# K transposed by VectorE in a one-core decode step (sliding attention beside a squared-ReLU MLP), and one w2 row laid on half the partitions

## The chip, the core and the metric

The kernel runs on one core of a Trainium2 chip. The core has five engines that run their own instruction streams and wait for one another through semaphores: TensorE (PE, matmuls; its weight loads are listed as PEld), VectorE (DVE), ScalarE (ACT), GpSimd (POOL) and SyncE (SP, which here only issues loads). Sixteen DMA engines move data between the main memory and the on-chip memory SBUF; matmul results go to PSUM. The metric is device time in microseconds (us), as the median of several runs; lower is better.

## What is computed

For two sequences with one new token each: a layer norm, attention of 32 query heads over the last 2048 positions of a cache with 16 K/V heads, and an MLP with a squared ReLU; both read the same normed token, and both are added to the input.

```python
W = min(4096, max(256, Sk // 4))                  # Sk = 8192: W = 2048
xn = _layernorm(x, axis=-1)                       # x: (2, 1, 576), bf16
q = (xn @ wq).reshape(B, Sq, 32, 128)             # wq: (576, 4096)
k = repeat(k_cache[:, :, Sk - W:, :], 2)          # caches: (2, 16, 8192, 128)
v = repeat(v_cache[:, :, Sk - W:, :], 2)
p = softmax(einsum("bhqd,bhkd->bhqk", q, k) * 128 ** -0.5)
a = einsum("bhqk,bhkd->bhqd", p, v).reshape(B, Sq, 4096) @ wo
h = relu(xn @ w1 + b1)                            # w1: (576, 4608)
m = (h * h) @ w2 + b2                             # w2: (4608, 576)
out = x + a + m
```

## The kernel before

**Units.** The attention is cut into eight units, u = 0 to 7; a unit is one sequence with four K/V heads. Its K and its V are 2 MB each. In SBUF a K tile has 128 partitions (four heads by 32 groups of 64 positions) and in each partition 64 rows of 128 bf16 numbers. Two bf16 numbers next to each other are moved as one f32, so a row is 64 f32.

**Loads.** All large loads are issued by SP, and they run in the order of issue: K0, wq, K1, V0, K2, V1, K3 at the start; V2, K4 and so on from the loop, each as soon as its buffer is free. K and V tiles share six buffers (`kvpool`), taken in turn; wq, w1 and wo share one buffer (`wbig`). So K4 waits until unit 1's K has been transposed, V3 until unit 0's V has been used, and wo until the matmuls with w1 (`mlp_h`) are done. w2 is split in two halves (x = 0, 1) of 18 rows for each partition; the first half goes to `w2a`, the second to `w2b` (9 rows, in a K/V buffer) and to `w2c` in pieces of 6, 2 and 1 rows (`W2P`), the last loads of the kernel. The small loads of x, b1 and b2 are issued from ScalarE's queue.

**A unit's work** (`step(u)`, line 387). `transposes(u, g)` (line 258) runs eight times: four 128x128 f32 transposes on TensorE into PSUM, and one copy to SBUF, by ScalarE (line 270) or VectorE (line 272) in turn. `scores(u, t)` (line 274), for either half t of the K tile, is eight matmuls of 512 columns whose stationary tile has 32 columns; four of them stand beside one another in the array (`tile_position`) and write to different partitions of `sc_ps`. The stationary tile is a window into `qz`, in which q stands between zeros. A first matmul puts a very low number at scores of foreign heads. `softmax(u)` (line 288) takes the maximum of each partition (VectorE), the maximum over partitions (GpSimd's `partition_all_reduce`), the exponential (ScalarE) and a transpose in 32x32 blocks to `pT` (VectorE). `pv(w)` (line 314), for the unit w = u - 2, is sixteen matmuls; `pv_end(w)` (line 326) adds the four column groups on VectorE, and its inner `fin` does one more matmul, the division by the sum, and writes the output of the heads to `ws`.

**Order.** TensorE's instructions keep the order of the program: the helpers `matmul` and `transpose` (lines 93 and 96) pass each through `keep_in_program_order`. Those of VectorE, ScalarE and SP are ordered by the tile framework, which also places all semaphore waits. The program's order is: transposes of unit 0, `q_block` (line 226: q = xn @ wq, transposed and laid into `qz`), scores and softmax of unit 0, steps 1 to 6, `mlp_h` (line 356), loads of wo and w2, step 7, the values of units 6 and 7, and at last the output matmuls (`out_acc`): 128 with wo, 72 with `w2a`, 36 with `w2b`, 36 with `w2c`; then one copy and the store.

Of the kernel before, what the change touches and what calls it, by code (L numbers as in the profile page):

```python
# [16 lines left out]
def kernel(  # L17
# [14 lines left out]
    nc = tc.nc  # L32
# [17 lines left out]
    JG = 8  # L50
    NG = NJ // JG
# [5 lines left out]
    TG = NG // NT  # L57
    QZ = 2 * NC
    assert SR == 32 and NG % NT == 0

# [15 lines left out]
    W2P = [(9, 15), (15, 17), (17, 18)]  # L76
    R9 = 9
# [15 lines left out]
    def matmul(*a, **k):  # L93
        tc.keep_in_program_order(nc.tensor.matmul(*a, **k))  # L94

# [20 lines left out]
    def issue_flat(w, name):  # L116
        n = w.shape[0] * w.shape[1] // P
        tl = wbig.tile([P, NH * L1], BF16, tag="wbig", name=name)
        nc.sync.dma_start(out=tl[:, 0:n], in_=w.rearrange("r n -> (r n)").rearrange("(p l) -> p l", p=P))
        return tl  # L120

    const.tile([P, 144], F32, name="pad_0")
# [15 lines left out]
    tmp_f = work.tile([P, 2, Dh], F32, tag="tmp", name="tmp_f")  # L138
# [50 lines left out]
    nc.vector.tensor_scalar(out=off[:], in0=own[:], scalar1=BIG, scalar2=-BIG, op0=ALU.mult, op1=ALU.add)  # L189
    of_h = const.tile([P, NC * WC], F32, name="of_h")  # L190
# [20 lines left out]
    w2c_sb = w2pool.tile([P, (FR - R9) * D], BF16, name="w2c")  # L211
# [8 lines left out]

    qz = const.tile([P, NQ, B, 2, 3 * QZ], BF16, name="qz")
    nc.gpsimd.memset(qz[:], 0.0)
# [3 lines left out]
    def q_block():  # L226
        for t in range(NH):
            for g in range(NG4):
                o = t * LQ + g * QW
                matmul(q_ps[32 * g:32 * g + 2 * B, :], lhsT=xnT[:, t].rearrange("p x b -> p (x b)"),  # L230
                       rhs=wq_sb[:, o:o + QW], start=(t == 0), stop=(t == NH - 1), skip_group_check=True,
                       tile_position=(0, 32 * g))
        row_t = const.tile([RB, 4 * HW], BF16, tag="row", name="qrow")
        qrow = row_t[:, 0:2 * QW]
        nh = QH // 2
        for k in range(2):
            cp = nc.scalar.copy if k else nc.vector.tensor_copy
            cp(out=qrow[:, k * QW:(k + 1) * QW].rearrange("p (i a d) -> p i a d", a=2, d=Dh),  # L238
               in_=q_ps[0:RB, k * QW // 2:(k + 1) * QW // 2].rearrange("p (i d) -> p i d", d=Dh).unsqueeze(2)
               .to_broadcast([RB, nh, 2, Dh]))  # L240
        qrow_f = qrow.bitcast(F32)
        qT_ps = psum.tile([P, QH * P], F32, tag="sc", bufs=2, name="qT_ps")
        for i in range(QH):
            transpose(out=qT_ps[:, i * P:i * P + RB], in_=qrow_f[:, i * Dh:(i + 1) * Dh],
                      identity=ident_f[0:RB, 0:RB])
        qT_v = qT_ps[:].bitcast(BF16).rearrange("p (i g e x b c) -> p b x g c e i", g=NG4 // 2, e=2, x=32 // B, b=B, c=2)
        hd = Dh // 2
        for j2 in range(2):
            cp = nc.scalar.copy if j2 else nc.vector.tensor_copy
            pp = slice(hd * j2, hd * (j2 + 1))  # L250
            o = QZ + NC * j2
            for b in range(B):
                for half in range(2):
                    cp(out=qz[pp, half * NQ // 2:(half + 1) * NQ // 2, b, :, o:o + NC].rearrange(  # L254
                        "p g c (e i) -> p g c e i", e=2), in_=qT_v[pp, b, half])

    kT_tiles, sc_tiles, pT_tiles, o1_tiles, o_tiles = {}, {}, {}, {}, {}
    def transposes(u, g):
        k_f = k_tiles[u][:].bitcast(F32)
        kT_ps = psum.tile([P, JG * P], BF16, tag="kT", bufs=3, name=f"kT_ps_{u}_{g}")  # L260
        kT_f = kT_ps[:].bitcast(F32)
        for i in range(JG // 2):
            j = g * JG // 2 + i
            transpose(out=kT_f[:, i * P:(i + 1) * P], in_=k_f[:, j * P:(j + 1) * P], identity=ident_f[:])
        t, o = divmod(g, TG)
        if o == 0:
            kT_tiles[(u, t)] = ktpool.tile([P, TG * JG * P], BF16, tag="kT_sb", name=f"kT_{u}_{t}")
        kT = kT_tiles[(u, t)][:, o * JG * P:(o + 1) * JG * P]
        if g % 2 == 0:
            nc.scalar.copy(out=kT, in_=kT_ps[:])  # L270
        else:
            nc.vector.tensor_copy(out=kT, in_=kT_ps[:])  # L272

    def scores(u, t):
        tq, b = divmod(u, B)
# [4 lines left out]
        kT = kT_tiles.pop((u, t))[:].rearrange("p (j k c) -> p j k c", k=P, c=2)  # L280
        z = QZ * (1 - t)
        for c in range(2):
            for g in range(4):
                matmul(sc_ps[32 * g:32 * (g + 1), :], lhsT=qz[:, tq, b, c, z:z + SR],
                       rhs=kT[:, :, 32 * g:32 * (g + 1), c], start=False, stop=(t == NT - 1 and c == 1),
                       skip_group_check=True, tile_position=(0, 32 * g))

    def softmax(u):
        sc_ps = sc_tiles.pop(u)
        m1 = work.tile([P, 1], F32, tag="m1", name=f"m1_{u}")  # L290
        nc.vector.tensor_reduce(out=m1[:], in_=sc_ps[:], axis=AX.X, op=ALU.max)  # L291
        m2 = work.tile([P, NC], F32, tag="m2", name=f"m2_{u}")
        nc.vector.tensor_scalar(out=m2[:], in0=off[:], scalar1=m1[:, 0:1], scalar2=None, op0=ALU.add)  # L293
        gmax = work.tile([P, NC], F32, tag="gmax", name=f"gmax_{u}")
        nc.gpsimd.partition_all_reduce(gmax[:], m2[:], channels=P, reduce_op=ReduceOp.max)  # L295
        gown = work.tile([P, NC], F32, tag="gown", name=f"gown_{u}")
        bias = work.tile([P, 1], F32, tag="bias", name=f"bias_{u}")
        nc.vector.scalar_tensor_tensor(out=gown[:], in0=gmax[:], scalar=-scale, in1=own[:], op0=ALU.mult,  # L298
                                       op1=ALU.mult, accum_out=bias[:])
        p_sb = work.tile([P, NJJ * 32], BF16, tag="p_sb", bufs=1, name=f"p_{u}")  # L300
        o1 = keep.tile([P, Dh + 1], F32, tag="o1", name=f"o1_{u}")
        nc.scalar.activation(out=p_sb[:], in_=sc_ps[:], func=ACT.Exp, bias=bias[:, 0:1], scale=scale,  # L302
                             accum_out=o1[:, Dh:Dh + 1])
        pT = keep.tile([P, NJJ, SR], BF16, tag="pT", name=f"pT_{u}")
        nc.vector.transpose(out=pT[:].rearrange("p j r -> p (j r)"), in_=p_sb[:])  # L305
        pT_tiles[u] = pT
        o1_tiles[u] = o1
# [4 lines left out]
    nc.gpsimd.memset(hT_sb[:], 0.0)  # L312

    def pv(u, part, parts):
        n = NJJ // parts
        if part == 0:
            o_tiles[u] = psum.tile([P, NS * Dh], F32, tag="o", name=f"o_ps_{u}")
        v = v_tiles[u][:].rearrange("p (t j s d) -> p j t s d", t=NT, s=2, d=Dh)
        for j in range(part * n, (part + 1) * n):
# [3 lines left out]
        if part == parts - 1:  # L323
            pT_tiles.pop(u)

    def pv_end(u):
# [3 lines left out]
        for k in range(NS):  # L330
            kw = dict(out=o1[:, 0:Dh], in0=o_ps[:, k * Dh:(k + 1) * Dh])
            if k == 0:
                nc.vector.tensor_scalar(scalar1=in_s[:, 0:1], scalar2=None, op0=ALU.mult, **kw)  # L333
            else:
                nc.vector.scalar_tensor_tensor(scalar=in_s[:, k:k + 1], in1=o1[:, 0:Dh], op0=ALU.mult, op1=ALU.add,  # L335
                                               **kw)

        def fin():
# [5 lines left out]
            nc.vector.reciprocal(out=linv[pp, :], in_=op[pp, Dh:Dh + 1])  # L344
            om_t = work.tile([P, Dh], F32, tag="om", name=f"om_{u}")
            om = om_t[pp, :].rearrange("p (q r) -> p q r", r=WR)
            nc.vector.scalar_tensor_tensor(out=om, in0=op[pp, 0:Dh].rearrange("p (q r) -> p q r", r=WR),
                                           scalar=linv[pp, 0:1], op0=ALU.mult, op1=ALU.mult,
                                           in1=own_c[pp, :].unsqueeze(2).to_broadcast([32, WC, WR]))
            with nc.allow_low_precision(reason="sums of one term and zeros"):  # L350
                nc.vector.tensor_reduce(out=ws[pp, :, BS * b], in_=om.rearrange("p q r -> p r q"), axis=AX.X,
                                        op=ALU.add)
# [3 lines left out]
    def mlp_h(w1_sb):  # L356
        h_ps = [psum.tile([P, HB], F32, tag="kT", bufs=3, name=f"h_ps_{k}") for k in range(2)]
# [28 lines left out]

    def step(u):
        fin = None
        w = u - 2
        with_pv = w >= 0  # L390
        for g in range(NG):
            transposes(u, g)
            if with_pv and g == 1:
                pv(w, 0, 2)
            if with_pv and g == 2:
                pv(w, 1, 2)
                fin = pv_end(w)
            if g == TG + 1:
                scores(u, 0)
            if g == TG + 2 and fin:  # L400
                fin()
        scores(u, 1)
        softmax(u)

    def pv_all(u):
        pv(u, 0, 1)
        pv_end(u)()

    for g in range(NG):
        transposes(0, g)  # L410
    q_block()
    for t in range(NT):
        scores(0, t)
    softmax(0)
    load_v(2)
    b1_rows = B_b1.rearrange("(x n) -> x n", n=HW)
    for i0, i1 in ((0, 2), (2, 4), (4, 6), (6, 8)):
# [3 lines left out]
    load_k(4)  # L421
# [16 lines left out]
    nc.sync.dma_start(out=w2a_sb[:], in_=w2_rows[0])  # L438
# [10 lines left out]
    for r in range(FR):  # L449
        w, o = (w2b_sb, r) if r < R9 else (w2c_sb, r - R9)  # L450
        out_acc(hT_sb[:, 1, r, :], w, o, stop=(r == FR - 1))
# [36 lines left out]
```

## Time and profile before

| what | value |
|---|---|
| median of 7 runs | 133.96 us (133.94 to 134.53) |
| the profiled execution: its own time, its span | 133.98 us, 132.1 us |
| loads from main memory | 53.6 MB, 406 GB/s over the span |
| mean granted clock of TensorE | 0.84 of full speed |
| last wq byte landed, first scores | 19.1 us, 25.6 us |
| last K tile (unit 7) issued, transposed | 61.3 us, 108 us |
| wo issued, after the w1 matmuls | 95.0 us |
| last `ws` ready, end of the wo matmuls | 118.2 us, 122.0 us |
| `w2a`, `w2b`, first piece of `w2c` landed | 122.8, 125.9, 128.0 us |
| last matmul, end of the span | 129.3 us, 132.1 us |

The span is the time from the first to the last instruction in the trace of one execution; the time of that execution is some 2 us longer. A page shows the busy time of each engine, the span in 40 slices (each digit is a busy share in tenths), the chain of work that ended last, and groups of like instructions. In a group, the arrow shows output and inputs by the program's names; "x32" is the number of instructions; then come the busy time in us, the mean time of one in ns, and the idle time of the engine just before them with what ended it. [...]

### The profile page before, as it was taken

The numbers are of one execution on the slowest core, as the hardware profiler recorded it, in microseconds if no ns is written. First come the engines' busy times: TensorE is split into PE (matmuls) and PEld (weight loads), VectorE is DVE, ScalarE is ACT, GpSimd is POOL, SyncE is SP. The second block draws the span as 40 slices with busy tenths as digits, with TensorE's granted clock in tenths as the row PEclk, the third lists the DMA queues.
The fourth block names the chain that finished last, engine by engine and source line by source line (L and its number), as shares of the span: only waits on it lengthen the run. The fifth ranks groups of instructions, "written<-read, shape, count | busy, mean of one in ns | idle before, by whom it ended". The sixth has DMA issues, their size and how long they took to land.

```text
span 132.1 us, 2285 instructions
## 1 busy us (share of the span) xinstructions
PE 84.9 (64%) x949; PEld 52.0 (39%) x949; DVE 63.4 (48%) x176; ACT 46.7 (35%) x67; POOL 4.9 (4%) x15
## 2 busy tenths in 40 slices
PE   0079229599589687597599779304739974339561
PEld 0069102276345353263436435002436631128450
DVE  7764300345657677396527757620165377750000
ACT  5716300339576094373253376020206352000000
POOL 5000000010010100100100010100000001000000
PEclk9999985959999999999658999975775699856955
DMA  4999899999999999999999999999999999899960
GB/s 150 407 437 514 380 393 427 432 437 427 434 412 446 422 437 422 432 437 422 442 427 414 437 488 402 427 454 387 432 427 446 463 413 480 376 408 430 408 253 1
DMA packets 3511, 53.76 MB, mean 407 GB/s; under 512 B 419, under 2 KB 558, under 8 KB 814
## 3 DMA queue, kind: packets, MB, share of 16 engines
q1 hardware_dynamic: 3456, 53.61, 95.1%
q8 instruction: 7, 0.11, 0.3%
q10 hardware_dynamic: 46, 0.02, 0.1%
q14 instruction: 2, 0.02, 0.0%
HBM read 53.62 MB, written 0.00 MB: 406 GB/s over the span
## 4 chain that ended last, share of the span: by engine, by line
DMA 78%; PE 15%; ACT 2%; SPq 1%; DVE 1%; issue 1%; ACTq 0%; DVEq 0%
DMA w<-in_B_w_dram 25%; DMA w2c<-in_B_w_dram 24%; DMA k<-in_A_k_cache_dram 16%; DMA wq<-in_A_wq_dram 13%; PE kT_ps L97 5%; PE h_ps L94 3%; PE q_ps L94 3%; PE sc_ps L94 2%; PE out_ps L94 1%; PE o_ps L94 1%; ACT kT L270 1%; DVE qrow L238 1%; SPq L106 0%; ACT qrow L238 0%; DVE qz L254 0%
## 5 line engine op out<-in xcount | busy, mean ns | idle before, releaser
L97 PE MATMUL kT_ps<-ident_f,k 128*128 128x128 f32 x256 | 41.8, 313 | 6.4 <-DMA k<-in_A_k_cache_dram 4.1
L97 PEld LDWEIGHTS kT_ps<-ident_f,k 128*128 128x128 f32 x256 | 32.8, 161 | 21.2 <-issue 12.1
L270 ACT COPY kT<-kT_ps 128x1024 bf16<-128x1024 bf16 x32 | 31.9, 1012 | 20.4 <-PE kT_ps L97 20.2
L272 DVE COPY kT<-kT_ps 128x1024 bf16<-128x1024 bf16 x32 | 21.8, 682 | 6.3 <-PE kT_ps L97 6.1
L94 PE MATMUL sc_ps<-kT,qz 128*32 128x512 bf16 x128 | 10.3, 406 | 6.7 <-DVE kT L272 4.7
L302 ACT ACTIVATE p<-sc_ps,bias 128x512 bf16<-128x512 f32 x8 | 5.5, 687 | 21.4 <-DVE gown L298 21.4
L94 PE MATMUL o_ps<-v,pT 128*32 128x512 bf16 x128 | 11.4, 442 | 0.0
L94 PEld LDWEIGHTS <-xnT 128*4 128x4 bf16 x108 | 3.4, 115 | 15.4 <-issue 14.0
L305 DVE STREAM_TRANSPOSE pT<-p 128x512 bf16<-128x512 bf16 x8 | 5.7, 710 | 6.2 <-ACT p L302 6.2
L335 DVE SCALAR_TENSOR_TENSOR o<-o_ps,in_s,o 128x128 f32<-128x128 f32 x24 | 8.3, 345 | 0.4
L94 PE MATMUL h_ps<-w,xnT 128*4 128x288 bf16 x72 | 3.9, 397 | 6.8 <-DMA w<-in_B_w_dram 6.8
L291 DVE TENSOR_REDUCE m<-sc_ps 128x1 f32<-128x512 f32 x8 | 5.5, 692 | 5.3 <-PE sc_ps L94 5.3
L295 POOL PARTITION_ALL_REDUCE gmax<-m x8 | 2.9, 367 | 105.8 <-DVE m L293 105.8
L94 PE MATMUL q_ps<-wq,xnT 128*4 128x512 bf16 x36 | 3.8, 596 | 4.8 <-DMA wq<-in_A_wq_dram 4.8
L94 PE MATMUL op_ps<-o,of_h 128*32 128x129 f32 x16 | 3.4, 299 | 4.8 <-DVE o L335 4.8
L375 DVE TENSOR_TENSOR hrow<-t 100x1152 bf16<-100x1152 f32 x2 | 2.6, 1355 | 8.0 <-ACT t L373 8.0
L94 PEld LDWEIGHTS <-qz 128*32 128x32 bf16 x128 | 2.2, 96 | 10.5 <-DVE kT L272 7.2
L456 ACT CAST fin_sb<-out_ps 113x144 bf16<-113x144 f32 x1 | 0.3, 279 | 17.0 <-PE out_ps L94 17.0
L97 PE MATMUL pro_ps<-ident,xn_sb 2*128 2x2 bf16 x5 | 0.9, 181 | 6.8 <-DVE xn_sb L171 6.5
L333 DVE TENSOR_SCALAR o<-o_ps,in_s 128x128 f32<-128x128 f32 x8 | 2.7, 343 | 5.0 <-PE o_ps L94 4.9
L94 PEld LDWEIGHTS <-hT_sb 128*17 128x17 bf16 x144 | 3.5, 111 | 3.8 <-issue 3.7
L238 DVE CAST qrow<-q_ps 100x512 bf16<-100x512 f32 x1 | 0.7, 691 | 7.9 <-PE q_ps L94 7.9
(71 smaller groups left out, 58.1 us busy)
## 6 DMA issues: line engine op xcount, KB each, us to landing
k<-in_A_k_cache_dram SPq DMA_DIRECT2D x8, 2048.0 KB, 21.0
v<-in_A_v_cache_dram SPq DMA_DIRECT2D x8, 2048.0 KB, 21.5
w<-in_B_w_dram SPq DMA_DIRECT2D x1, 5184.0 KB
wq<-in_A_wq_dram SPq DMA_DIRECT2D x1, 4608.0 KB, 17.7
wo<-in_A_wo_dram SPq DMA_DIRECT2D x1, 4608.0 KB
w2a<-in_B_w_dram SPq DMA_DIRECT2D x1, 2592.0 KB, 27.3
w2b<-in_B_w_dram SPq DMA_DIRECT2D x1, 1296.0 KB
w2c<-in_B_w_dram SPq DMA_DIRECT2D x1, 864.0 KB
```

The lines of the kernel that those rows point to most:

```text
L94: tc.keep_in_program_order(nc.tensor.matmul(*a, **k))
L97: tc.keep_in_program_order(nc.tensor.transpose(*a, **k))
L238: cp(out=qrow[:, k * QW:(k + 1) * QW].rearrange("p (i a d) -> p i a d", a=2, d=Dh), in_=q_ps[0:RB, k * QW // 2:(k + 1) * QW // 2].rearrang ...
L270: nc.scalar.copy(out=kT, in_=kT_ps[:])
L272: nc.vector.tensor_copy(out=kT, in_=kT_ps[:])
L291: nc.vector.tensor_reduce(out=m1[:], in_=sc_ps[:], axis=AX.X, op=ALU.max)
L295: nc.gpsimd.partition_all_reduce(gmax[:], m2[:], channels=P, reduce_op=ReduceOp.max)
L302: nc.scalar.activation(out=p_sb[:], in_=sc_ps[:], func=ACT.Exp, bias=bias[:, 0:1], scale=scale, accum_out=o1[:, Dh:Dh + 1])
L305: nc.vector.transpose(out=pT[:].rearrange("p j r -> p (j r)"), in_=p_sb[:])
L333: nc.vector.tensor_scalar(scalar1=in_s[:, 0:1], scalar2=None, op0=ALU.mult, **kw)
L335: nc.vector.scalar_tensor_tensor(scalar=in_s[:, k:k + 1], in1=o1[:, 0:Dh], op0=ALU.mult, op1=ALU.add, **kw)
L375: nc.vector.tensor_tensor(out=h4[:, :, k * HB:(k + 1) * HB], in0=t4, in1=t4, op=ALU.mult)
```

## The change

**K is transposed by VectorE.** In `transposes(u, t)`, now called twice for a unit, one VectorE instruction turns half a K tile, 128 partitions by 2048 f32, in blocks of 32x32: within each group of 32 partitions, straight from SBUF to SBUF. TensorE's 32 transposes of a unit, their PSUM tiles and the eight copies are gone.

**Scores with a block-diagonal stationary tile.** After that, each group of 32 partitions holds other positions, and one matmul has to multiply each group by q alone. `own_p` marks the group of each partition. `q_block` lays q, four times over the partitions, into `qc`; for each unit `q_place(u)` multiplies `qc` by `own_p` into one of two tiles `qz`, which makes it block-diagonal. A stationary tile is now a 128-column window into `qz`, and `scores(u, t)` is eight matmuls over the whole array, with 512 columns each.

**The order on VectorE is written out.** VectorE's instructions of a unit go through `keep_in_program_order` (`dve`). In `step(u)`: `pv(u - 2)` and both halves of the scores on TensorE; on VectorE `pv_end(u - 2)`, the maxima of unit u, `fin`, `q_place(u + 1)`, the first transpose of unit u + 1, then `rest` (bias, exponential on ScalarE, `pT`), then the second transpose of unit u + 1.

**Loads.** K4 is loaded before step 1 instead of after it, b1 in eight loads instead of four; wq, w1, wo and `w2a` keep the order of the program. `w2b` holds 11 rows and `w2c` 6 (pieces of 3, 2 and 1). The 18th row of the second half of w2 goes to a tile `w2x` on partitions 0 to 63, two rows on each, in four loads between `w2a` and `w2b`; for it `mlp_h` makes the matching part of h (`hx_sb`) by one more transpose and three ScalarE copies, and eight output matmuls take the place of four.

The core of the diff:

```diff
-    W2P = [(9, 15), (15, 17), (17, 18)]
-    R9 = 9
+    R9 = 11
+    RL = FR - 1
+    W2P = [(R9, 14), (14, 16), (16, RL)]
+    PL = P // 2
...
+    dve = tc.keep_in_program_order
...
-    qz = const.tile([P, NQ, B, 2, 3 * QZ], BF16, name="qz")
-    nc.gpsimd.memset(qz[:], 0.0)
+    qc = const.tile([P, NQ, B, NA, NC], BF16, name="qc")
+    qz = [const.tile([P, NA, P + QO], BF16, name=f"qz_{k}") for k in range(2)]
+    for k in range(2):
+        nc.gpsimd.memset(qz[k][:], 0.0)
...
+        for h in range(2):
+            cp = nc.scalar.copy if h else nc.vector.tensor_copy
+            cp(out=qrow[:, h * 2 * QW:(h + 1) * 2 * QW].rearrange("p (i a d) -> p i a d", a=NP4, d=HD),
+               in_=q_v[:, h].unsqueeze(2).to_broadcast([RB, QH, NP4, HD]))
...
+    def q_place(u):
+        tq, b = divmod(u, B)
+        sh = [P, NA, NP4, NC]
+        dve(nc.vector.tensor_tensor(out=qz[u % 2][:, :, QO:].rearrange("p a (q c) -> p a q c", c=32)[:, :, :, 0:NC],
+                                    in0=qc[:, tq, b].unsqueeze(2).to_broadcast(sh),
+                                    in1=own_p[:].unsqueeze(1).unsqueeze(3).to_broadcast(sh), op=ALU.mult))
...
-    def transposes(u, g):
...
-        for i in range(JG // 2):
-            j = g * JG // 2 + i
-            transpose(out=kT_f[:, i * P:(i + 1) * P], in_=k_f[:, j * P:(j + 1) * P], identity=ident_f[:])
...
-        if g % 2 == 0:
-            nc.scalar.copy(out=kT, in_=kT_ps[:])
-        else:
-            nc.vector.tensor_copy(out=kT, in_=kT_ps[:])
+    def transposes(u, t):
+        kT = ktpool.tile([P, UE // NT], BF16, tag="kT_sb", name=f"kT_{u}_{t}")
+        n = UE // NT // 2
+        tc.keep_in_program_order(nc.vector.transpose(out=kT[:].bitcast(F32),
+                                                     in_=k_tiles[u][:].bitcast(F32)[:, t * n:(t + 1) * n]))
+        kT_tiles[(u, t)] = kT
...
-        for c in range(2):
-            for g in range(4):
-                matmul(sc_ps[32 * g:32 * (g + 1), :], lhsT=qz[:, tq, b, c, z:z + SR],
-                       rhs=kT[:, :, 32 * g:32 * (g + 1), c], start=False, stop=(t == NT - 1 and c == 1),
-                       skip_group_check=True, tile_position=(0, 32 * g))
+        for i in range(NS // NT):
+            z = QO - NC * (t * NS // NT + i)
+            for h in range(2):
+                for e in range(2):
+                    matmul(sc_ps[:], lhsT=qz[u % 2][:, 2 * h + e, z:z + P], rhs=kT[:, i, :, h, :, e], start=False,
+                           stop=(t == NT - 1 and i == NS // NT - 1 and h == 1 and e == 1), skip_group_check=True)
...
     def step(u):
...
+        if w >= 0:
+            pv(w)
+        for t in range(NT):
+            scores(u, t)
+        fin = pv_end(w) if w >= 0 else None
+        rest = softmax(u)
+        if fin:
+            fin()
+        if u + 1 < NU:
+            q_place(u + 1)
+            transposes(u + 1, 0)
+        rest()
+        if u + 1 < NU:
+            transposes(u + 1, 1)
...
+    q_place(0)
+    step(0)
     load_v(2)
+    load_k(4)
...
-    for i0, i1 in ((0, 2), (2, 4), (4, 6), (6, 8)):
+    for i0, i1 in tuple((i, i + 1) for i in range(8)):
...
+    w2_last = w2_rows[1, :, RL * D:FR * D].rearrange("(e i q j) n -> e i j q n", e=2, i=2, q=4)
+    for i in range(2):
+        for e in range(2):
+            nc.sync.dma_start(out=w2x_sb[32 * i:32 * (i + 1), e, :], in_=w2_last[e, i])
     nc.sync.dma_start(out=w2b_sb[:], in_=w2_rows[1, :, 0:R9 * D])
```

## The prediction, made before the changed kernel was run

> **What bounds the kernel now.** I read the page's first two parts, then the chain that ended last, then the timeline of one unit, then the groups by shape. The page's head and the chain in order of time (start us, us, what):
>
> ```profile
> span 132.1 us, 2285 instructions
> PE 84.9 (64%) x949; PEld 52.0 (39%) x949; DVE 63.4 (48%) x176; ACT 46.7 (35%) x67; POOL 4.9 (4%) x15
> DMA  4999899999999999999999999999999999899960
> ...
> 58.08 32.97 DMA w<-in_B_w_dram
> ...
> 96.35 31.57 DMA w2c<-in_B_w_dram
> ...
> 127.96 1.36 PE out_ps L94 x36
> ```
>
> No engine is full; the DMA row stands at 9 from the second slice to the last but one, and the chain is 78% DMA. The kernel is bound by its load stream: 53.6 MB at about 430 GB/s. One unit's K and V (4.19 MB) take 9.8 us of it, and the compute of a unit fits in. The slack is small at the end: the last `ws` is ready at 118.19, the 128 `wo` matmuls end at 122.0, and `w2a` lands at 122.8. A compute end some 3 us later takes the bound over. So the question is whether a unit still fits in 9.8 us when VectorE (DVE) does all the transposing. One unit's softmax now (start us, us):
>
> ```profile
> 45.47 0.37 POOL L295 PARTITION_ALL_REDUCE gmax<-m  x1 [8.59 <-DVE m L293]
> 45.87 0.17 DVE L298 SCALAR_TENSOR_TENSOR gown<-gmax,own 128x8 f32<-128x8 f32 x1 [0.57 <-POOL gmax L295]
> 46.17 0.69 ACT L302 ACTIVATE p<-sc_ps,bias 128x512 bf16<-128x512 f32 x1 [3.15 <-DVE gown L298]
> 46.98 0.71 DVE L305 STREAM_TRANSPOSE pT<-p 128x512 bf16<-128x512 bf16 x1 [0.93 <-ACT p L302]
> ```
>
> From `gown` to the end of pT it is 47.69 - 45.87 = 1.82 us, 0.93 of it DVE's wait for the exponential. The groups (busy us, mean ns):
>
> ```profile
> L97 PE MATMUL kT_ps<-ident_f,k 128*128 128x128 f32 x256 | 41.8, 313 | 6.4 <-DMA k<-in_A_k_cache_dram 4.1 <-ACT kT L270 2.2
> L270 ACT COPY kT<-kT_ps 128x1024 bf16<-128x1024 bf16 x32 | 31.9, 1012 | 20.4 <-PE kT_ps L97 20.2
> L272 DVE COPY kT<-kT_ps 128x1024 bf16<-128x1024 bf16 x32 | 21.8, 682 | 6.3 <-PE kT_ps L97 6.1
> L305 DVE STREAM_TRANSPOSE pT<-p 128x512 bf16<-128x512 bf16 x8 | 5.7, 710 | 6.2 <-ACT p L302 6.2
> L144 DVE STREAM_TRANSPOSE row<-tmp_f 128x32 f32<-128x32 f32 x1 | 0.2, 163 | 0.0
> L375 DVE TENSOR_TENSOR hrow<-t 100x1152 bf16<-100x1152 f32 x2 | 2.6, 1355 | 8.0 <-ACT t L373 8.0
> L238 DVE CAST qrow<-q_ps 100x512 bf16<-100x512 f32 x1 | 0.7, 691 | 7.9 <-PE q_ps L94 7.9
> ```
>
> **Removed.** 256 TensorE transposes (41.8 us), 32 ScalarE copies (31.9) and 32 DVE copies (21.8). None lies long on the chain, so this buys nothing by itself. DVE gives up 4 x 0.68 = 2.7 us a unit.
>
> **Added on DVE: two transposes of 128x2048 f32 a unit.** The trace has no such size. L238 to L375 gives DVE's pace: (1355 - 691)/(1152 - 512) = 1.04 ns an element. L305 carried on at that pace: 710 + 1536 x 1.04 = 2.30 us. The line through the two transposes (163 at 32, 710 at 512) has 1.14 ns and gives 2.46. As a floor, the L272 pace (682 for 1024) gives 1.36; as a ceiling, twice the pace from L144 gives 163 + 2016 x 2.08 = 4.36. I take 2.30, nearest the same operation, and 2.34 with the gap.
>
> [...]
>
> **DVE's order is now written out**, so a step is a sum. From the end of the second transpose of unit u: `pv_end`, four operations, 114.92 to 116.43 in the timeline, 1.51. Then the wait for the second eight score matmuls, below. m1 and m2, 0.69 + 0.23 + gaps, 1.0. `fin`, 0.16 + 0.35 + 0.40 + gaps, 0.97. `q_place`, 128 elements; the nearest row is L347 with 347 ns, 0.38 (bounds 0.2 to 0.5). First transpose 2.34. `rest`, 1.82 + 0.04. Second transpose 2.34. The POOL reduction hides under `fin` and the first transpose; the exponential is waited for, and behind pT stands the second transpose, for which TensorE waits. Without the scores wait: 1.51 + 1.0 + 0.97 + 0.38 + 2.34 + 1.86 + 2.34 = 10.4 us, already above 9.8.
>
> **The scores wait.** 32-column matmuls ran four beside each other; the new ones fill the array and run singly: 16 a unit, 512 columns each. `q_ps` ran four abreast in 3.76/9 = 0.42 us at granted clock 0.5, so one takes 0.42 at half clock and 0.21 at full. Eight and 0.2 of latency are 1.9 or 3.6 us, of which `pv_end` covers 1.5: the wait is 0.4 or 2.1. Which clock? Stretches (length, PE, PEld, DVE, ACT, POOL busy, clock, DMA share, GB/s):
>
> ```profile
> 60.05:63.46 3.41, 1.85 (x17) 0.75 (x15) 2.30 (x5) 1.01 (x1) 0.00 (x0) 1.00 0.99 423
> 63.46:66.87 3.41, 2.48 (x16) 1.71 (x16) 1.61 (x5) 1.73 (x3) 0.37 (x1) 0.50 1.00 428
> 66.87:70.29 3.42, 3.42 (x25) 1.88 (x18) 0.90 (x3) 1.07 (x2) 0.00 (x0) 0.50 1.04 434
> 111.26:114.67 3.41, 1.17 (x18) 0.57 (x18) 2.68 (x10) 0.78 (x2) 0.00 (x0) 1.00 0.94 405
> ```
>
> The clock changed at steps of 3.41 us: it fell after a stretch with 1.85 us busy, stayed low after 2.48, and came back after 3.42. In the new step TensorE at full clock has 8 x 0.21 + 0.2 scores, 0.4 `op`, 1.2 pv, then some 3 us of nothing until the first transpose, 2.1 of scores, and 2 of nothing. So the clock will fall in most steps, and return when the doubled work fills a stretch. I take the middle: a step of 11.6, between 10.8 and 12.5.
>
> [...]
>
> **The start.** `qrow` now has 1024 columns a half: DVE 0.69 + 512 x 1.04 = 1.22, ScalarE 1.01 by L270's row, one after the other as now: +0.95. Two more transposes +0.2; `q_place` +0.38; the first half's copies move under ScalarE's, -0.5. Scores of unit 0 begin at 25.64 + 1.05 = 26.7. Seventeen matmuls at full clock take 3.7, at half 7.2; the clock was 0.5 from 25.9 on, so I put the end at 33.6, against 27.3 now. Then 1.0 + 0.38 + 2.34 + 1.86 + 2.34 = 7.92: unit 1 transposed at 41.5. Step 1 has no `pv_end` to cover the wait (1.9 or 3.6, say 2.7): 41.5 + 2.7 + 7.92 = 52.1. Five steps of 11.6: unit 7 transposed at 110.1. K itself is there in time throughout (unit 7's at about 96).
>
> **The end.** `hrow` and its 2.63 us (95.34 to 97.97) fall among DVE's last steps. Scores 2.7. m1 to pT end 3.36 (109.76 to 113.12). To the last `ws` 5.07 (113.12 to 118.19). `wo` matmuls 3.6. The w2 matmuls, 148 for 144, by 1.05 + 0.77 + 1.26 + 1.34 = 4.42: 4.54. Sum 21.9: TensorE ends at 132.0 against 129.32, +2.7. With the 2.78 behind it the span is 134.8. Around the span lies 133.98 - 132.1 = 1.9, and 133.98 is the median (133.96) but for 0.02: 136.7.
>
> **Queues.** `wo` waits for the `w1` matmuls, which stand on TensorE behind step 6: transposed at 98.5, + 3.6 + 0.6, + 3.9 as now = 106.6. Loads queued behind w1 (landing 91.1) are 6.3 MB, dry at 105.7. The stream loses 1 to 3 us there and ends near 131: no more than the compute. K and V buffers come free later too (K of unit 5 issued at 52 instead of 42.9), but each stays some 10 us ahead of its place in the stream. Eight `b1` loads for four: 4 x 0.33 us on ScalarE's queue ahead of `rstd`; what follows from it is wanted at 19.1 and done by 8.4; without that cover 1.3. They also held SP's issues up (6.3 us in three waits), under 9 MB of loads queued since 2.25.
>
> **The w2 row.** Same bytes, four SP issues of 0.42 us, 25 us ahead of their data. In the last 1.3 us before 128.5 the DMA share is about 0.4: part of the engines are done. [...] Bounds -0.4 to +0.5 with small packets; only worth something while the stream is the bound, so 0 here. The extra `hx` transpose and three ScalarE copies (about 0.31 each) hide while DVE transposes unit 7; uncovered 1.2.
>
> **Rivals.** *The stream stays the bound* (0.35). One mechanism: clock at full in the first scores (-3) and in the steps (10.8: -4.0) brings the chain to 125 to 128, before the data; from 3 us on it decides. Then the w2 row and a steadier stream count: 132.8 to 134.2, likeliest 133.4, faster. For it: before.py's compute of a unit is only 9 us, K is always early, and half the steps may run at full clock. Against: 10.4 without any wait.
> *Half clock throughout* (0.12): steps of 12.5 add 4.5: 141.2. For it, the long idle stretches; against, doubled work fills them.
> *The f32 transpose runs at half pace* (0.03): 14 transposes stand after 33.6, x 2.06 = 29 us: 165. Against it: L144 leaves then only 96 ns fixed, below the 130 ns and more of other small operations.
> The forecast has 0.50. [...]
>
> **Numbers.** 136.7; faster 0.26, same 0.07 and slower 0.02 share the first rival's 0.35; slower is 0.50 + 0.12 + 0.03 + 0.02 = 0.67. A measurement of this kernel tells 0.2% from no change. Range 132.8 to 140.5: the first rival whole, steps up to 12.3; the likeliest case's own 134.5 to 139.
>
> **What will show it.** Transposes of 2.2 to 2.5 us, 16 of them; steps, from one second transpose to the next, of 10.8 to 12.5; DVE the largest share of the chain in place of DMA; the clock at 0.5 in much of 30 to 110; `wo` issued after 103; dips of the DMA row near slice 32. I am wrong if steps are under 10.5 or the chain is still mostly DMA.

## The result, and the profile after

The changed kernel takes 1.017 times the time of the kernel before (95% interval 1.0147 to 1.0193), 2.3 us more on 134.03. The profiled execution took 135.84 us. The median of all twelve executions, 138.16 us, includes some at a lower granted clock of TensorE (0.78 to 0.80 of full speed), which the comparison leaves out; 1.017 stands for about 136.3 us. So the change made the kernel slower, close to the 136.7 that was forecast, but much of the agreement is two errors that cancel, as the sections below show.

The page of the changed kernel, its head, the busy rows, the chain by engine and the new transposes:

```profile
span 134.0 us, 1753 instructions
...
PE 70.6 (53%) x702; PEld 31.0 (23%) x702; DVE 81.3 (61%) x169; ACT 16.4 (12%) x38; POOL 5.5 (4%) x17
...
PEclk9999999959999999689689689779975579755698
DMA  4999899999999999999999999999999999999920
...
DMA 35%; DVE 27%; PE 26%; ACT 4%; issue 4%; SPq 1%; ACTq 0%
...
L274 DVE STREAM_TRANSPOSE kT<-k 128x2048 f32<-128x2048 f32 x16 | 36.5, 2284 | 0.0
```

TensorE lost 14 us of work, ScalarE 30, and VectorE gained 18. The chain was 78% DMA before and is 35% now. The DMA row is still at 9 until the data are all there, near 128.7. Behind that TensorE works on: compute ends this kernel, not the stream. The clock row shows 6 8 9 three times from the 17th slice on: once in each step the clock is halved, from 1.00 to 0.50 in the stretches below.

The chain of the same kernel in order of time (start us, us, what) from the landing of w1:

```profile
62.53 29.64 DMA w<-in_B_w_dram
...
92.21 2.28 PE h_ps L96 x68
...
94.96 2.63 DVE hrow L381 x2
...
101.48 2.19 DVE kT L274
...
104.66 1.83 PE o_ps L96 x16
106.48 5.14 PE sc_ps L96 x17
...
117.51 1.94 PE o_ps L96 x14
...
127.39 1.82 issue
129.21 1.98 PE out_ps L96 x99
```

From its issue at 62.53 up to 92.17 the chain is the load of w1, as before (58.08 to 91.05): the steps on VectorE were in time for `w1`, since unit 6 was transposed at 89.5. Everything behind it is new. Unit 7 is transposed at 103.67, but its first score matmul starts at 106.48, because on TensorE the transposes of h, `hx` and pv(5) stand in front. Then 17 scores run in one row, 5.14 us, those up to 109.0 at half clock, and pv(7) does not begin before 117.5. The last `ws` is ready at 122.76, against 118.19 before.

The clock in stretches of one step of the same kernel (length, PE, PEld, DVE, ACT, POOL busy, clock, DMA share, GB/s):

```profile
57.84:61.25 3.41, 2.85 (x23) 1.22 (x25) 2.71 (x6) 0.00 (x0) 0.00 (x0) 1.00 1.01 432
61.25:64.66 3.41, 0.96 (x10) 0.28 (x3) 3.31 (x7) 0.00 (x0) 0.37 (x1) 1.00 1.01 432
64.66:68.07 3.41, 3.09 (x8) 1.11 (x8) 2.48 (x5) 0.78 (x2) 0.00 (x0) 0.50 1.01 432
```

A stretch with 0.96 us of work is followed by one at half clock, which the first eight scores fill; the next is at full clock again, and the second eight scores run in it. From unit 2 on a step, from one second transpose to the next, is 10.1 to 10.3 us here, three stretches of 3.41.

### The profile page after: what moved, and what is told of

The parts are those of the page before. It is cut to its first block, busy times and chain, and to the rows that moved or that the text cites. A ratio compares the mean times of both kernels' runs of the same rounds, so it can differ in the third digit from the quotient of the medians.

```text
span 134.0 us, 1753 instructions
## 1 busy us (share of the span) xinstructions
PE 70.6 (53%) x702; PEld 31.0 (23%) x702; DVE 81.3 (61%) x169; ACT 16.4 (12%) x38; POOL 5.5 (4%) x17
## 4 chain that ended last, share of the span: by engine, by line
DMA 35%; DVE 27%; PE 26%; ACT 4%; issue 4%; SPq 1%; ACTq 0%
DMA w<-in_B_w_dram 22%; DMA wq<-in_A_wq_dram 13%; DVE kT L274 13%; PE sc_ps L96 12%; PE out_ps L96 5%; PE o_ps L96 4%; PE q_ps L96 3%; ACT p L307 3%; DVE pT L310 3%; DVE m L294 2%; DVE hrow L381 2%; PE h_ps L96 2%; DVE o L341 2%; PE op_ps L96 1%; DVE qrow L248 1%
## 5 line engine op out<-in xcount | busy, mean ns | idle before, releaser
L96 PE MATMUL sc_ps<-kT,qz 128*128 128x512 bf16 x128 | 38.6, 457 | 23.2 <-DVE gown L303 16.8
L274 DVE STREAM_TRANSPOSE kT<-k 128x2048 f32<-128x2048 f32 x16 | 36.5, 2284 | 0.0
L96 PEld LDWEIGHTS <-qz 128*128 128x128 bf16 x128 | 14.1, 111 | 46.2 <-issue 32.3
L96 PE MATMUL o_ps<-v,pT 128*32 128x512 bf16 x128 | 11.6, 443 | 0.0
L248 DVE CAST qrow<-q_ps 100x1024 bf16<-100x1024 f32 x1 | 1.2, 1225 | 9.9 <-PE q_ps L96 9.9
L96 PEld LDWEIGHTS <-pT 128*32 128x32 bf16 x128 | 4.2, 105 | 5.5 <-issue 3.9
L101 PE MATMUL hp<-ident,hrow 100*128 100x100 bf16 x18 | 1.7, 255 | 5.4 <-DVE hrow L381 3.1
L96 PE MATMUL out_ps<-wo,ws 128*17 128x144 bf16 x128 | 3.7, 307 | 1.2 <-DVE ws L357 1.2
L96 PEld LDWEIGHTS <-ws 128*17 128x17 bf16 x128 | 3.5, 129 | 1.6 <-issue 1.6
L96 PEld LDWEIGHTS op_ps<-o,of_h 128*32 128x32 f32 x16 | 1.2, 115 | 9.9 <-issue 9.5
L248 ACT CAST qrow<-q_ps 100x1024 bf16<-100x1024 f32 x1 | 1.0, 1012 | 18.7 <-DVE qrow L248 18.7
(77 smaller groups left out, 53.6 us busy)
```

The lines of the kernel that those rows point to most:

```text
L101: tc.keep_in_program_order(nc.tensor.transpose(*a, **k))
L248: cp(out=qrow[:, h * 2 * QW:(h + 1) * 2 * QW].rearrange("p (i a d) -> p i a d", a=NP4, d=HD), in_=q_v[:, h].unsqueeze(2).to_broadcast([RB, ...
L274: tc.keep_in_program_order(nc.vector.transpose(out=kT[:].bitcast(F32), in_=k_tiles[u][:].bitcast(F32)[:, t * n:(t + 1) * n]))
```

## The experiments

Three theories at first. T: the loss is in the hand-over at unit 7. S: the load stream runs late and sets the end. D: VectorE's eight steps set the end, as forecast. "After" and "before" are the two kernels of the change; ratios are against the kernel before, on the same chip. `T(7,0)` and `T(7,1)` in the expectations are unit 7's two transposes.

**pv_end(6) inside the wait for unit 7's exponential** (in after):

```diff
-    pv_all(NU - 2)
+    pv(u - 1)
+    rest(lambda: pv_end(u - 1))()
```

> Changed kernel, with the four operations that add up unit 6's values (pv_end) moved into VectorE's wait for the last exponential, and unit 6's pv ahead of it on TensorE. Theory T (the loss is made in the hand-over at unit 7: MLP work, last transposes, single score matmuls and a fixed VectorE order, all after w1 has landed): the values of unit 7 start 1.5 us earlier, the last ws comes at about 121.3 instead of 122.75, the last matmul at 129.7 instead of 131.2, time 134.2 to 134.7 against 135.9. Rival S (the load stream is late at the end and sets it): less than 0.3 us. Rival D (the eight VectorE steps set the end, as the prediction had it): also -1.5, so this run parts S from the others.

135.98 us, ratio 1.0134 (1.0077 to 1.0191), a smaller gain than T and D expected. The last `ws` is ready at 121.44 in its profile and not at 122.76, but the last matmul comes only 0.75 us sooner. The end of its chain says why:

```profile
96.28 27.05 DMA w2x<-in_B_w_dram
...
123.35 6.80 DMA w2c<-in_B_w_dram
...
130.19 0.27 PE out_ps L96 x4
```

With the compute a little shorter the stream decides: SP issues the last piece of w2 only when a half-row load, issued 27 us before, has landed. T and S seem both to have a part; the interval overlaps with that of after, so this run settles no size.

**The squares and copies of h on ScalarE** (in after; `...` stands for the unchanged operands):

```diff
-            nc.vector.tensor_tensor(out=h4[...], in0=t4, in1=t4, op=ALU.mult)
+            nc.scalar.activation(out=h4[...], in_=t4, func=ACT.Square)
-                cp = nc.scalar.copy if g % 2 else nc.vector.tensor_copy
+                cp = nc.scalar.copy
```

> Changed kernel, with the MLP's squares (hrow) and all copies to hT_sb on ScalarE, so that VectorE has only attention work between w1's landing and the scores of unit 7. Theory T: the first transpose of unit 7 starts when its K lands (96 to 97 instead of 97.5), the second ends near 102.5, scores of unit 7 end at 106.5 to 108 instead of 111.6, the last ws comes at 117.5 to 119.5, and then the data set the end again: last matmul 129.0 to 129.6, time 133.6 to 134.3. Rival D (VectorE's chain as a whole): the 2.6 us of the squares and 1.2 of copies off VectorE, time 132.5 to 133.5. Rival S: no change.

136.62 us, ratio 1.0197 (1.0165 to 1.0229): a miss. Its timeline (start us, us, engine, line, operation; in brackets the idle time before, and its releaser) shows where the 2.63 us went:

```profile
99.10 2.21 ACT L381 ACTIVATE hrow<-t 100x1152 bf16<-100x1152 f32 x2
...
102.22 1.27 ACT L390 COPY hT_sb<-hp 32x36 bf16<-32x36 bf16 x4 [0.53 <-PE hp L101]
...
104.33 0.71 DVE L310 STREAM_TRANSPOSE pT<-p 128x512 bf16<-128x512 bf16 x1 [4.16 <-ACT p L307]
```

The exponential of unit 6 was now behind squares and copies in ScalarE's queue, and VectorE stood 4.16 us in front of pT with the last transpose of K behind it. The wait was moved, not removed.

**The w2 row alone** (in before): `R9 = 11`, pieces of 3, 2 and 1 rows, the four half-row loads, `h_last` and `hx`, and nothing else of the change.

> Kernel before, with only the change of w2: one row of the second half on partitions 0 to 63, w2b with 11 rows, w2c with pieces of 3, 2 and 1, and hx with its copies. There the data set the end. [...] Rival (small loads cost): 0.3 to 0.6 slower by their packets. [...]

135.35 us, ratio 1.0104 (1.0082 to 1.0126). More than the 0.3 to 0.6 us put for small loads; where it comes from is taken up below, with the run on the whole row.

**Steps 2 to 5 without fin** (in after; the division and the `ws` rows of units 0 to 3 are not computed):

```diff
-        if fin:
+        if fin and u > 5:
             fin()
```

> Changed kernel that leaves out fin (one matmul and three VectorE operations, 0.97 us a step) in steps 2 to 5, so that the parts of the result of units 0 to 3 are missing. Rival D (VectorE's steps set the end): 4 steps x 0.97 = 3.9 us earlier, time 132 to 133. Theory T: the second transpose of unit 6 ends at about 85.6 instead of 89.5, but the MLP still waits for w1 at 92.2, so the end moves by less than 0.5 us; time 135.4 to 136.2 at an equal clock in the tail. Rival S: no change either.

136.44 us, ratio 1.0164 (1.0125 to 1.0203). Some 1 us less of work in each of four steps, and no gain. The steps of its profile took turns of 10.9 and 9.2 us: what was saved came back as waits for the scores, 2.27 us of VectorE in the long turns against 0.6 in the short. D in its plain form falls: in after, unit 6 was transposed 2.7 us before `w1` had landed.

**After with w2 as before** (18 ordinary rows; the four half-row loads, `h_last` and `hx` are gone):

```diff
-    RL = FR - 1
-    W2P = [(R9, 14), (14, 16), (16, RL)]
+    RL = FR
+    W2P = [(R9, 15), (15, 17), (17, RL)]
```

> The changed kernel with w2 loaded and multiplied as before (18 ordinary rows, pieces 4/2/1 from row 11). Theory H (after the hand-over at unit 7 the end is set by VectorE and TensorE; the loads have landed 2.5 us before the last matmul): the row's loads were hidden, the time stays at that of the changed kernel, 1.012 to 1.020 of the kernel before, the last ws write stays at 122 to 125 us and the last matmul near 131. Theory W (the row's loads, which alone cost 1.4 us on the kernel before, cost as much here): 1.4 us less than the changed kernel, ratio 1.004 to 1.009, last matmul near 129.8.

Ratio 1.0152 (1.0116 to 1.0188): as after. **The same with pv_end(6) in the wait:**

> The kernel of the run before with pv(6) put ahead of the wait for unit 7's exponential and its pv_end inside that wait. Both losses are taken away together. Theory H+W (the hand-over at unit 7 and the row's loads each hide behind the other): less than either alone, ratio 0.998 to 1.008, last ws write 120.5 to 122, last matmul 128.8 to 130. If the hand-over alone decides: as the first experiment, ratio 1.010 to 1.017. If PE's clock or its fetch of instructions decides: no change from the changed kernel, ratio 1.015 to 1.02.

Ratio 1.0205 (1.0157 to 1.0254): no better than either alone. Its six executions lie at two granted clocks, 0.797 to 0.800 with 137.28 to 138.15 us, and 0.842 to 0.858 with 136.31 to 136.64. In the profiled one (0.797) unit 7 was transposed at 109.6 and the last matmul ended at 132.3; after's profile, at 0.856, has 103.67 and 131.19.

**Filler matmuls for the clock** (in after), 87 of this one: 8 in each step ahead of the scores, 9 behind each block of the transposes of h, 14 and 7 at the end.

```diff
+            matmul(idle_ps[:], lhsT=far_h[:], rhs=is_h, start=True, stop=True, skip_group_check=True)
```

> The changed kernel with 87 matmuls more that nobody reads (128x512, into a bank of their own): 8 ahead of each unit's scores from unit 1 to 6, 9 behind each block of the transposes of h, 14 and 7 ahead of the last two sums over rows. They are there for the clock alone. Theory C (the half clock of scores(7), pv(7) and wo costs 4 to 5 us at the end): these run at full clock, 17 scores of unit 7 in 2.7 to 3.7 us and not 5.1, the run ends 1 to 3 us sooner, ratio 0.995 to 1.010. Rival (the fillers' own time, 0.22 to 0.44 us each, is on the path of every step, and VectorE's turns of 10.2 us grow): each step 1.7 to 3 us longer, ratio 1.02 to 1.08. The pause of TensorE near the end comes 174 instructions earlier in the program's own order, if it is a fetch of instructions in blocks.

Ratio 1.0389 (1.0334 to 1.0444). The fillers in the hand-over ran on the path, mostly at half clock, 3.1 + 3.95 + 3.1 us. Those in the steps were free: steps stayed at 10.1 to 10.3 us. But they did not hold the clock up either. Two stretches of its profile:

```profile
62.50:65.92 3.42, 2.42 (x14) 0.85 (x10) 3.35 (x8) 0.00 (x0) 0.36 (x1) 1.00 1.01 431
65.92:69.33 3.41, 3.38 (x8) 1.11 (x8) 2.48 (x4) 0.78 (x2) 0.00 (x0) 0.50 1.03 442
```

2.42 us of busy time in 3.42 were followed by half clock. Busy time alone does not decide it, though, as two stretches of after show, where 1.50 us were followed by full clock:

```profile
37.36:40.77 3.41, 1.50 (x7) 0.57 (x6) 2.06 (x1) 0.00 (x0) 0.00 (x0) 1.00 1.01 430
40.77:44.18 3.41, 2.06 (x24) 0.71 (x23) 2.74 (x4) 0.00 (x0) 0.36 (x1) 1.00 1.04 442
```

The 1.50 us are scores, which multiply over 128 partitions; of the 2.42 us, 1.90 are the eight fillers, which multiply over 4. Whether that makes the difference was not shown: no run varied their shape. The pause of TensorE that after has near the end (1.82 us in its chain) did not come 174 instructions earlier; this run had none there.

**VectorE's order left to the framework** (in after; the transposes of K too):

```diff
-    dve = tc.keep_in_program_order
+    def dve(i):
+        return i
```

> The changed kernel with VectorE's order left to the framework (the writes of pv_end, the softmax and the transposes are not pinned). Theory O (the written order holds pT and the last two pv_end apart wrongly at the end, but keeps the steps short): steps of another length than 10.2 us, and the end follows them: ratio 1.00 to 1.012 if the order at the end was the loss, 1.02 to 1.06 if the order in the steps was the gain. If the order decides nothing: 1.014 to 1.020 as the changed kernel.

Ratio 1.0234 (1.0193 to 1.0275); the interval just touches that of after. The chain of its profile has all sixteen scores of a unit in one row, behind both transposes:

```profile
52.32 5.65 PE sc_ps L96 x16
...
64.36 6.45 PE sc_ps L96 x16
```

Steps of 12 to 13 us. In this profile the written order, with the second transpose beside the first eight scores, is worth its place in the steps.

**The hand-over rewritten** (after, with w2 as before). The loss at the end is that hrow stands ahead of unit 7's transposes and that the blocks of h and the scores share two banks. Now the squares go behind pT(7) and behind the last `ws`, and the transposes and copies of h (`mlp_t`) behind the `wo` matmuls; `mlp_h` keeps the matmuls and the Relu:

```diff
-    mlp_h(w1_sb)
+    hrow, square = mlp_h(w1_sb)
...
+    fin = rest(lambda: pv_end(u - 1))
+    square(0)
+    fin()
+    pv_all(u)
+    square(1)
     for r in range(WR):
         out_acc(ws[:, r, :], wo_sb, r)
+    mlp_t(hrow)
```

> The changed kernel with w2 as in the kernel before, and with the rest of the MLP behind the scores of unit 7: the two squares of h between the softmax of unit 7 and its end, the transposes of h and their copies behind the wo matmuls, pv(6) and its pv_end inside the waits of unit 7's softmax. Theory H (the loss is the hand-over: 17 scores of unit 7 wait until 106.5 for the transposes of h, which hold the two score banks, and hrow is ahead of the last transposes): scores(7,0) begin with T(7,0), near 98, the last ws write comes at 110 to 116 and not at 122 to 125, the end goes back to the loads: last matmul 128.5 to 130, ratio 0.994 to 1.004. Theory D (VectorE's eight turns set the end): T(7,1) ends 100 to 104 and the end is little earlier, ratio 1.008 to 1.018. Theory C (the granted clock decides): its low executions stay 2 to 4 us longer than the others, as those of the changed kernel; under H they lie within 0.6 us, since the chain then has 8 to 10 us to spare.

**The same on after itself**, with the row on 64 partitions:

> The same with the w2 row on 64 partitions, as in the changed kernel. If the row's four small loads cost the stream as they did alone (1.4 us), they are now in sight: ratio 0.008 to 0.012 over that of the run before, last w2 piece landing near 130. If they were hidden in any case, or cost only with the kernel before: the same ratio as the run before within 0.004.

136.66 us, 1.0197 (1.0178 to 1.0217), for the first; 134.92 us, **1.0062 (1.0043 to 1.0081)**, for the second, which differs from after in the hand-over alone. So after loses 1.1%, some 1.4 us, by its hand-over. Neither expectation of the second held, as it came out faster than the first; and for the first H's ratio was missed. With w2 as before the rewriting gained nothing (1.0152 without it). The second also has no pause of TensorE near the end; the 1.82 us that the pause takes in after's chain are more than the 1.4, and no run parts the pause from the waits of the hand-over. All six executions of the second lie within 134.46 and 135.23, at clocks from 0.79 to 0.87: the dependence on the clock is gone. Its timeline:

```profile
99.60 2.31 DVE L274 STREAM_TRANSPOSE kT<-k 128x2048 f32<-128x2048 f32 x1
...
101.96 1.90 PE L96 MATMUL sc_ps<-kT,qz 128*128 128x512 bf16 x8 [0.40 <-DVE gown L303]
...
103.51 2.27 DVE L274 STREAM_TRANSPOSE kT<-k 128x2048 f32<-128x2048 f32 x1
...
105.83 1.90 PE L96 MATMUL sc_ps<-kT,qz 128*128 128x512 bf16 x8 [1.97 <-DVE kT L274]
```

The scores now follow each transpose at once. Unit 6 was transposed 6 us later than in after's profile (95.4 and not 89.5), and still the last `ws` was ready at 117.6, 5 us sooner. `wo` was issued at 100.4, and the stream, summed over stretches of 5 us, had moved 46.30 MB by 110 us against 46.45 before: the late issue cost it almost nothing. What ends this run is a load again:

```profile
104.33 23.44 DMA w2b<-in_B_w_dram
127.81 2.46 PE out_ps L96 x67
```

`w2b` has 11 rows here and not 9, and landed at 127.77, against 125.9 before; 67 matmuls stand behind it, where the kernel before has 36 behind its last load (1.36 us).

In the first of the two the chain goes back to the stream, but to a late one:

```profile
101.32 29.72 DMA w2c<-in_B_w_dram
131.08 0.68 PE out_ps L96 x12
```

Its last data landed at 131.04, against 127.92 for the kernel before. T was right about the hand-over; what it uncovered was S. Two causes of the late stream then came in sight.

**The row whole, on before**: pieces and order as in the run of the row alone, but the 18th row as one load over 128 partitions.

```diff
-    W2P = [(9, 15), (15, 17), (17, 18)]
-    R9 = 9
+    R9 = 11
+    RL = FR - 1
+    W2P = [(R9, 14), (14, 16), (16, RL)]
...
+    nc.sync.dma_start(out=w2x_sb[:], in_=w2_rows[1, :, RL * D:FR * D])
     nc.sync.dma_start(out=w2b_sb[:], in_=w2_rows[1, :, 0:R9 * D])
```

> The kernel before with the changed pieces and order of w2 alone (rows 0 to 10, then 3, 2 and 1), and the 18th row issued ahead of them as one load over all 128 partitions. If the 64 partitions and the four loads are what cost 1.4 us: 133.9 to 134.4, ratio 0.998 to 1.003. If it is the order (a small load ahead, whose completion the last pieces wait for on SP): 135.0 to 135.6, ratio 1.007 to 1.012.

134.29 us, 1.0016 (1.0004 to 1.0029). So order and pieces cost next to nothing, and it looks as if the 64 partitions, or the four loads, cost 1.4 us. The stream says otherwise. From 25 to 95 us, before any w2 load is issued, the row-alone run is already slower than the kernel before. Stretches of the two (columns as above), before first:

```profile
0.00:25.00 25.00, 11.64 (x78) 7.55 (x78) 10.40 (x44) 9.08 (x11) 1.97 (x7) 0.93 0.92 390
25.00:95.00 70.00, 51.58 (x479) 29.71 (x478) 38.23 (x97) 30.62 (x44) 2.57 (x7) 0.88 1.01 430
```

```profile
25.00:95.00 70.00, 50.93 (x461) 29.09 (x463) 38.47 (x98) 30.53 (x43) 2.56 (x7) 0.86 1.00 427
```

The DMA engines are busy all the time in both (shares of 1.01 and 1.00); they move less. Over all runs there are two classes, and they follow the address at which the framework put the K and V tiles (the traces don't show addresses; these are sums of the sizes of the tiles in the source):

| kernel | first K tile at byte | GB/s, 25 to 95 us |
|---|---|---|
| before; row whole | 31232 | 430; 431 |
| after; pv_end(6) in the wait; ScalarE; without fin; order free; fillers; hand-over with row | 32768 | 431, the fillers 430 |
| row alone | 31456 | 427 |
| after with w2 as before; the same with pv_end(6); hand-over, w2 as before; the last run below | 32544 | 428 |

Taking `hx_sb` and `h_last` out or in shifts every later tile by 224 bytes. The two tiles themselves are not the cause: with them after runs at 431 and the row alone at 427, without them before runs at 430 and after with w2 as before at 428. At 427 for 430 GB/s the 53.6 MB take 0.9 us longer (53.6/0.427 - 53.6/0.430). That is most of the row's 1.4 us. The rest can be the last piece, which this run too issues at 123.61, when a half-row load has landed. The slower class burdens the experiments, not the change: after's tiles lie at 32768 (with a pad that the diff shortens by 128 bytes, `pad_0`), and its rate is 431. No run changed the address alone.

The two classes lie 0.5 to 0.9% apart; no run shows where in the transfer that arises, or why the two rates go with these addresses.

**b1 in four loads, the row whole, the hand-over rewritten** (after otherwise). In after SP's issue of K 1 waited for a b1 load. The waits of SP's queue (waiter, releaser: us in total, times, longest) in after, and then in this run:

```profile
SPq L110 <- DMA b_sb<-in_B_b_dram: 14.2, 1, 14.2
```

```profile
SPq L110 <- DMA b_sb<-in_B_b_dram: 6.4, 3, 2.3
```

```diff
-    for i0, i1 in tuple((i, i + 1) for i in range(8)):
+    for i0, i1 in ((0, 2), (2, 4), (4, 6), (6, 8)):
```

> The kernel of the run with hand-over and row, with two more edits: b1 in four loads as before (in the changed kernel eight, and SP's load of k 1 waits 14.2 us for one of them), and the 18th w2 row as one load over 128 partitions. Theory B (the eight b1 loads hold SP's queue, and the loads fall 0.2 to 0.4 MB behind between 16 and 25 us and never make it up): k 1 issued near 2.3 us and not 16, 9.70 to 9.76 MB moved by 25 us and not 9.35 to 9.52, last matmul 129.2 to 129.8, ratio 0.997 to 1.003. Rival (VectorE's steps free the K and V slots late, or the wo load is issued late): the loads as before at 25 us, but 0.2 to 0.5 MB behind by 105 us, ratio 1.004 to 1.010.

135.21 us, 1.0082 (1.0066 to 1.0097), all six within 135.03 and 135.33: the ratio that the rival expected. B's first part is confirmed all the same. K 1 is issued at 2.07 and not at 16.2, and the first 25 us move more again. After, then this run:

```profile
0.00:25.00 25.00, 5.31 (x45) 1.97 (x45) 12.64 (x41) 4.96 (x7) 2.58 (x9) 1.00 0.92 381
```

```profile
0.00:25.00 25.00, 5.09 (x44) 1.88 (x45) 12.67 (x41) 4.84 (x7) 2.38 (x8) 1.00 0.92 388
25.00:95.00 70.00, 48.14 (x211) 16.78 (x210) 46.38 (x81) 7.12 (x18) 2.19 (x6) 0.73 1.01 428
```

381 for 390 GB/s are 0.22 MB, 0.5 us that after never makes up; 388 are nearly all of it. Over all profiles, the four kernels with four b1 loads moved 388 to 390 GB/s in these 25 us and the ten with eight moved 368 to 385, so the 0.5 us can be 0.2 to 1.3. B's time did not come: the second line has the rate of the slower class, 428 GB/s, which takes back 0.9 us (53.6/0.428 - 53.6/0.431). The rival, slots freed late by slow steps, is not what lowers it: the hand-over with row has steps as long (11.3 us) and 431 GB/s. The steps of this execution, at a clock of 0.792, are seen in its chain:

```profile
50.28 3.59 PE sc_ps L96 x8
...
59.78 2.21 DVE kT L274
62.03 2.92 PE sc_ps L96 x8
...
83.97 3.58 PE sc_ps L96 x8
```

Here the second eight scores also run at half clock, 2.4 to 3.6 us and not 1.9. Five steps from 39.3 to 95.9 us: 11.3 us each.

No version beat the kernel before. The likeliest one was not run: the rewritten hand-over with four b1 loads and the first K tile at 32768. By the rows above, 134.92 less 0.5, it is an estimated 134.4 us, still no gain.

Left open: the two hand-over runs differ by 1.7 us, of which the address would explain 0.9; the first also moved 374 GB/s and the second 380 in the first 25 us, with the same loads, which is 0.35 us.

## Why the prediction was right, and where it was wrong

- **The verdict and its reason hold in outline; that the number came so close is luck.** Slower, because the compute behind the data grew past the stream. The rival "the stream stays the bound" is refuted for after by the chain, and "half pace" by the 2284 ns.
- **The transpose: right.** 2.30 us were put, 2.284 measured. So were eight scores, put at 1.9 or 3.6 us: 1.90 at full and 3.59 at half clock.
- **The clock: it was read rightly in outline, the step length was not, in the profiled execution.** It does fall after a stretch with little work and return after a full one (after 0.96 and 3.09 us of 3.41 in after's rows). How little is no fixed time: the prediction's row had it fall after 1.85 us of work, after kept it over stretches with 1.50 and 1.90. The step was put at 11.6 by the middle between a scores wait of 0.4 and 2.1. In after's profile the clock is back before the second scores, the wait is 0.5, and the step 10.2; by the prediction's own test (below 10.5) this term failed. In the last run, at 0.792, it is 11.3, and the steps of the two are written alike. What the prediction lacked is that a step of about three stretches (10.2 us, of 3.41 each) can keep its place in them. That the place of the first one decides which scores fall into a slow stretch is the author's reading of the two profiles; no run could set it.
- **Unit 7 transposed at 110.1: measured 103.67**, 6.4 us early. Unit 2 was transposed at 48.7 and not at 52.1 (3.4), four steps took 10.2 and not 11.6 (5.6), and the last took 14.2 (2.6 back), since it waited for `w1` and had hrow ahead of its transposes. `wo` was issued at 94.6 and not at 106.6, as unit 6 was ready before `w1` had landed. Where it came later (100.4), the stream lost almost nothing; the 1 to 3 us that were put for 106.6 are untested, since by the prediction the queue ran dry only at 105.7.
- **The tail from there, 21.9 us, was mis-sized: 27.5 measured.** The prediction let the scores of unit 7 start with the transposes and took the end's rows from the kernel before. Four things were missed: the scores wait 2.8 us for the transposes of h, `hx` and pv(5); all 17 then run in one row, those up to 109.0 at half clock (5.14 and not 2.7); the written order puts pv_end(6), then `op`, in front of pv(7) (7.3 and not 5.07 from pT to the last `ws`); and a pause of 1.82 us. The row of hrow, 2.63, lay ahead of the transposes, and the w2 matmuls were shorter, which takes part of it back. The hand-over run on after itself takes the first and third away, and the pause is gone with them: together 1.1% is regained.
- **131.2 for 132.0 at the last matmul is therefore -6.4 and +5.6**, luck and not a sum that was right.
- **The b1 loads at nothing: wrong by about 0.5 us in after's profile.** The cover named was 9 MB queued since 2.25 us; the eight loads were what kept K 1 from being queued until 16.2, so the cover was gone.
- **The w2 row at nothing: right for after.** Alone on before it measured 1.4 us, of which 0.9 go with the address of the tiles. The working counted four issues of 0.42 us and missed that the last piece waits for their landing; that stands in the chain as soon as compute ends earlier, as in the first run and in the row alone. What is left for it is at most some 0.5 us, by subtraction and not by a run. No run shows what its bounds of -0.4 to +0.5 us rest on; the 1.4 us lie outside them.
- **The account of the 2.3 us:** 1.4 the hand-over with the pause (shown together, by the run on after itself), 0.5 the b1 loads (the bytes shown, the time worked out), some 0.3 unassigned.

## What to carry to other kernels

Here 14 us of work taken off TensorE and 30 off ScalarE bought nothing under the load stream, and some 1.4 us went at the seam behind it: list what stands in front of the first instruction of the last unit on every engine and in every shared bank. A price of nothing because "loads are queued since then" has to be checked against the change itself: does it alter when they are queued (here K 1 at 16.2 us and not 2.25, some 0.5 us)? And an experiment that removes a small tile moves every later tile, here by 224 bytes; compare the transfer rate in a stretch that the edit can't touch (here 427 to 431 GB/s) before reading its time.

## What the hardware showed that was not expected

- From 25 to 95 us the load stream ran at 430 to 431 GB/s with the first K tile at byte 31232 or 32768, and at 427 to 428 with it at 31456 or 32544, in fourteen kernels without an exception. No run changed the address alone.
- TensorE's clock changes in stretches of 3.41 us, and the busy time in one does not alone decide the next: in after 0.96 us were followed by half clock and 1.50 us of scores over 128 partitions by full clock, while 2.42 us with 1.90 of fillers over 4 partitions were followed by half clock. Executions of one program differ by up to 1.8 us within the comparison (the run with pv_end(6) and w2 as before).
- A few small loads on ScalarE's queue held the issue of a 2 MB load on SP's queue for 14.2 us.
- TensorE paused near the end for 1.0 us in before and 1.82 in after, with nothing in the profile to wait for. By the stretch up to the end of the pause it stands behind 859 matmuls and 860 weight loads in before and in the row whole (859 and 859 in the row alone), and behind 603 and 603 in after, give or take one or two in four of its variants: a fixed place in the program. The trace's DMA rows bear on it: in before and in after one packet of 16 KB, of the queue that the page calls "instruction", moved 2.3 us before the pause ended (at 122.55 in before, 124.87; at 126.9 in after, 129.21). In the run without fin the last 276 output matmuls ran from 125.50 in one row, without a pause; nor was there one with the fillers, with w2 as before or with the hand-over rewritten. That TensorE waits there for its instructions is the author's reading; no run moved that packet on its own.
